# One chained attention, softplus layer and expert layer on one core: another order at the seam between the layers, and the first expert's weights split earlier, one piece a step

## The chip, the cores and the metric

The kernel runs on one core of a Trainium2 chip. The metric is the device time of one execution in microseconds (us). A core has five engines that run their own instruction queues in order and wait for one another by semaphores: PE (TensorE, matrix products), ACT (ScalarE), DVE (VectorE), POOL (GpSimd) and SP, which here does nothing but issue DMAs.

## The reference

Three layers are chained. The first is a gated linear attention: a state of 48 x 48 for each of 8 heads is decayed and updated at each of 768 positions. The second is a two-layer network over 3072 tokens (384 to 2048 and back), with softplus between. The third is a layer of 8 experts, of which each token takes at most one.

```
x = attention(q, k, v, f_logit)                  # 3072 tokens x 384
h = x @ w_in;  g = softplus(h);  x = g @ w_out   # 384 -> 2048 -> 384
do = (x @ w_skip) > 0;  e = argmax(x @ w_gate)   # which tokens, which expert
out = x;  out[do] += prob[e] * (relu(x @ w1[e]) @ w2[e])
```

All products are made to float32's precision: each operand is a high part of reduced precision plus a low part, and each product is three matrix products (high by high, high by low, low by high).

## The kernel before

**Units and steps.** The tokens of the softplus layer go in 12 units of 256. A unit has 8 steps, each for 256 of the 2048 hidden columns, so there are 96 steps, `s` = 0 to 95 (loop at the line `for s in range(-20, total)`). The names in the trace carry the step within the unit: `ph6` of the last unit but one is step 86. A step's work is spread over four engines:

- `up(s)`: 18 matmuls into the PSUM tile `ph` (L396). Two such tiles exist, so `up(s)` waits until `ph` of step s-2 has been read for the last time.
- `act_a(s)`: on ACT absolute value (L411), exponential (L412), plus one (L413); on DVE two operations (L415, L416). L416 is the last reader of `ph`.
- `act_b(s)`: the logarithm on ACT (L422) and a sum on POOL (L423).
- `act_c(s)`: on ACT the high part `gh` (L431), on DVE the low part `gl` (L432).
- `down(s)`: 12 matmuls (L443) from `gh` and `gl` into the accumulators `acc0` and `acc1`. It is put behind `up(s+2)`. Its first matmuls need `gh`, the third or the fifth needs `gl`.

Up to step 85 the attention of the next units runs in between. The last step of the last unit works in halves of 256 columns, with the sum on DVE.

**Routing.** When a unit is through, `Route` copies the accumulators out (L463), writes the output rows and the table `x_s` of rows to DRAM (L464, L490, SP), picks an expert for each token and ranks the tokens by two small matmuls `pr` (L502, L503). The two `scatter` calls (L511) then write token numbers into the DRAM array `table` by indirect DMAs of POOL, the second after the first has landed. For the last unit there is no scatter: `last_rank` and `last_ids` do it on the chip, by `pr`, the one-hot tiles `prow` and `pcol` (L526, L527), the product `pplace` (L533) and the lists `ids`.

**The first expert's tokens.** The expert with the most tokens comes first. Its number is known after step 80 (`set_turns`). `first_ids` reads the first 256 places of its list from `table` into `col` (L602, read on DVE at L604), two gathers of POOL fetch those rows (`xg`, L663), and `firsts.turn` transposes them on PE (`pxg`, L694) and splits them (L373, L374). `firsts` then runs in four steps of `up` (`phm`, L711) and `down` (`pom`, L756) with expert 0's weights, and its `pom` uses the accumulators' PSUM. `table_cols` reads the whole table into `rows` by 8 DMAs (L542) and transposes it on PE (`pids`, L547).

**Expert weights.** An expert has four quarters of 768 KB, numbered `n` = 4e to 4e+3: two of w1, two of w2. `w_load(n)` brings one to SBUF by an SP DMA (L630, `w<-in_moe_w_dram`). `w_split(n)` takes two more slots for its high and low parts, and `w_piece` makes half of a quarter at a time: a cast on ACT (L640) and a subtraction on DVE (L641), both 128 x 768. The raw quarter's slot comes free after its second piece. `wanted` is the list of loads and splits to come, and `feed(n)` starts all of its head for which slots are free and then makes up to `n` pieces.

**What sets the order.** The calls stand in program order, but the build orders each engine's instructions by a schedule of its own, which may hoist work. `pin` keeps an instruction in program order while `pinned` holds something. In the kernel before it does so only from the last unit's routing on, so the pieces of steps 87 to 95 may move.

Of the kernel before, what the change touches and what calls it, by code (L numbers as in the profile page):

```python
# [23 lines left out]
PIECES = 2  # L24
# [13 lines left out]
def gla_softplus_moe_kernel(  # L38
# [17 lines left out]
    NCH, PR, _ = q.shape  # L56
# [14 lines left out]
    STEPS = NF // 2  # L71
# [534 lines left out]


    pools = {"w": mw, "wp": wp}
    slots = [("w", f"w{i}") for i in range(4)]
    raw, w_hi, w_lo, taken = {}, {}, {}, {}  # L610
    pinned = []

# [4 lines left out]
    def w_tile(n, dt):  # L617
        slot = slots.pop(0)
        taken.setdefault(n, []).append(slot)
        return pools[slot[0]].tile([P, KD, F2 // 2] if n % 4 < 2 else [P, NF2 // 2, DM], dt, tag=slot[1], name=f"w{n}", bufs=1)  # L620
# [5 lines left out]
    def w_load(n):  # L626
        e, g = n // 4, n % 4
        raw[n] = w_tile(n, F32)
        src = (w1 if g < 2 else w2)[ds(expert_at[e], 1), g % 2].rearrange("o p c -> (o p) c")
        sy.dma_start(out=raw[n].rearrange("p a c -> p (a c)"), in_=src)  # L630

    def w_split(n):

        w_hi[n], w_lo[n] = w_tile(n, F32R), w_tile(n, F32R)
        return [(n, i) for i in range(PIECES)]
# [9 lines left out]
    wanted, pieces = [], []  # L645

    def feed(n):

        while True:
            while wanted and len(slots) >= (1 if wanted[0][0] == "load" else 2):  # L650
                what, q = wanted.pop(0)
                if what == "load":
                    w_load(q)
                else:
                    pieces.extend(w_split(q))
            if n <= 0 or not pieces:
                return
            w_piece(*pieces.pop(0))
            n -= 1
# [140 lines left out]
    if True:  # L800
        se.preload_act_table_set("natural_log_exp_and_others")
        a_load(0, "fkq")
        a_load(1, "f")
        load_w(0, (0,))
        a_load(1, "kq")
        a_load(0)
        a_load(1)
        load_w(0, (1,))
        load_w(1)
        a_load(2)  # L810
        setup()
        load_wsg()
        clear_routes()
        stages = tuple(zip(("load", "pre", "decay", "transpose", "score", "out"), STAGE_AT))
        todo = {}
        for c in range(NCH):
            for nm, off in stages:
                todo.setdefault(4 * (c + 1) + off - (SOONER[c] if c < len(SOONER) else 0), []).append((c, nm))
        ops = {"load": a_load, "pre": a_pre, "decay": a_decay, "transpose": a_transpose, "score": a_score,
               "out": a_out}  # L820
        order = {nm: i for i, (nm, _) in enumerate(stages)}

        def attention_step(s):
            for c, nm in sorted(todo.pop(s, []), key=lambda x: (x[0], order[x[1]])):
                ops[nm](c)

        routes = {}
        ROUTE = ((1, "evac"), (4, "logits"), (5, "choose"), (6, "rank"), (7, "scatter", 0))
        ROUTE_SOON = ((1, "evac"), (1, "logits"), (2, "choose"), (2, "rank"), (3, "scatter", 0), (3, "scatter", 1))

        def route_step(u, i):
            if u < 0 or u >= NU:
                return
            if i == 1:
                routes[u] = Route(ffns[u], u * UNIT, tid[:, u * CPU:(u + 1) * CPU], *([pools["pre"], cnt_last] if u == NU - 1 else []))
            for at, nm, *a in ROUTE if u < NU - 3 else ROUTE_SOON if u < NU - 1 else ():
                if at == i:
                    getattr(routes[u], nm)(*(a if nm != "rank" else [cnt_acc[:, 0, :]]))
            if i == 2 and 0 < u < NU - 2:
                routes[u - 1].scatter(1)  # L840

        ffns = {}

        def conv(s, j):
            if s in CONV_AT:
                g = CONV_AT.index(s)
                if j % 2:
                    conv_w(g, j // 2)
                if j == 3 and g + 2 < STEPS:
                    load_w(g + 2)  # L850
        total = NU * STEPS
        last_att = 4 * NCH - 2 - STEPS
        for s in range(-20, total):
            u, i = divmod(s, STEPS)
            conv(s, 0)
            if s > 0:
                pu, pi = divmod(s - 1, STEPS)
                ffns[pu].act_b(pi)
            conv(s, 1)
            if s >= 0:  # L860
                if i == 0:
                    ffns[u] = Ffn(xhl[u], FINE if u == NU - 1 else ())
                ffns[u].up(i)
            if s > 0:
                ffns[pu].act_c(pi)
            if s >= 0:
                ffns[u].act_a(i)
            conv(s, 2)
            attention_step(s + STEPS + 1)
            conv(s, 3)  # L870
            if s >= 2:
                pu, pi = divmod(s - 2, STEPS)
                ffns[pu].down(pi)
            route_step(u - 1, i)
            if s == total - 2 * STEPS:
                set_turns()
                for n in range(4):
                    w_load(n)
            if s == last_att:
                first.close()  # L880
                pools["pre"] = rest.enter_context(tc.tile_pool(name="pre", bufs=1, side="right", reuse_waits="tile"))
                slots += [("pre", f"w{i}") for i in range(5)]
                wanted += [("split", n) for n in range(4)] + [("load", n) for n in range(4, 12)] + [("split", n) for n in range(4, 8)]
                for e in range(2, E):
                    wanted += [("split", n) for n in range(4 * e, 4 * e + 4)]
                    if e + 1 < E:
                        wanted += [("load", n) for n in range(4 * e + 4, 4 * e + 8)]
            if u == NU - 1:
                slots.append(("wp", f"s{i}"))
                if pu == u and pi % 2:  # L890
                    slots.extend(("wp", f"s{STEPS + pi - 1 + n}") for n in range(2))
            if s > last_att:
                feed(PIECES if s <= last_att + 4 else 1)
            if s == last_att + 2:
                first_ids()
                firsts = Tiles(0, [id0[:, 0, t:t + 1] for t in range(2)], ("acc0", "acc1"))
                firsts.fetch([id0[:, 1, t:t + 1] for t in range(2)], NT - 2 * UNIT)
            if s == total - 4:
                table_cols()
                last_base()  # L900
            if s == total - 3:
                firsts.turn()
                flags()
# [91 lines left out]
    ffn_end = ffns[NU - 1]  # L995
# [10 lines left out]
    def last_rank():  # L1006
        last.rank(cnt_all)
        last.place()
# [2 lines left out]
        set_ids(last.placed())  # L1011
        flag_counts()

    later = [[(ffn_end.down, STEPS - 2)], [(last_down,)]]
    seq = [(w, i) for w in work for i in range(len(w.steps))]
    fetched, turned = 1, 1
    ffn_end.act_b(STEPS - 1)
    for at in range(len(seq) + 2):
        if at < len(seq):
            w, i = seq[at]  # L1020
            while pieces and pieces[0][0] <= 4 * w.e + (1 if i == 0 else 3):
                w_piece(*pieces.pop(0))
            now, then = w.steps[i]
            for f, *args in now:
                f(*args)
            if at == 0:
                ffn_end.act_c(STEPS - 1)
            turn_at = 0 if w.n == 1 else 3 if w is firsts else 2
        for _ in range(2 if len(later) > 1 and (at == 2 or (at > 2 and w.n == 2 and i)) else 1):
            for f, *args in later.pop(0) if later else ():  # L1030
                f(*args)
        if at < len(seq):
            later += then
        feed(FILL[at])
        if at == 1:
            last_rank()
        elif at == 2:
            last_ids()
        if at >= 2 and at < len(seq):
            k0 = work.index(seq[at][0])  # L1040
            while fetched < len(work) and fetched <= k0 + 1:
                work[fetched].fetch(work[fetched].cols)
                fetched += 1
            if turned == k0 + 1 and turned < fetched and i == turn_at:
                work[turned].turn()
                turned += 1
# [9 lines left out]
    with tc.If(some > 0, preferred_fallthrough_block=False), ExitStack() as gen:  # L1056
# [23 lines left out]
        for e in range(E):  # L1080
            n = nc.values_load(cnt[0:1, e:e + 1], min_val=0, max_val=NT)
            with tc.If(n > 0):
# [6 lines left out]
                with tc.For_i(0, (n + (P - 1)) // P, 1) as it:  # L1089
# [3 lines left out]
                    w = Tiles(e, [c[:, 1:2]], ("acc0",))  # L1093
# [75 lines left out]
```

## Time and profile before

| | us |
|---|---|
| three runs | 750.46, 752.81, 754.51 |
| median | 752.81 |
| the profiled execution | 751.03 |
| its span, first to last instruction | 749.3 |
| PE busy | 688.8 (92%) |
| DVE busy | 538.5 (72%) |
| ACT busy | 477.2 (64%) |
| POOL busy | 199.3 (27%) |

Times in the trace count from the start of the span. An engine's bracket, as in [0.98 <-DVE u L416], says how long it sat idle before the instruction and what ended that. [...]

### The profile page before, as it was taken

To read this page: it belongs to the slowest core of one execution; us is meant where nothing else is said; L and a number is where in the kernel's file an instruction comes from. 1 tells how busy PE (TensorE), PEld (TensorE's weight loads), DVE (VectorE), ACT (ScalarE), POOL (GpSimd) and SP (SyncE) were. 2 spreads that over 40 slices of the span, in tenths; PEclk is the share of its full clock that TensorE was granted. 3 is DMA by queue.
4 is the path that set the end of the run, shared out by engine and by line. 5 is a ranking of instruction groups with operands and counts; after the bars stand their busy time and mean duration, and the time that the engine had idled before them with its cause. 6 is when DMAs were issued, how large, how long until landed. Compare 5 with 4: busy or idle time off the path is not lost. (4 is left out here: it accounts for less than half of the span.)

```text
span 749.3 us, 15063 instructions
## 1 busy us (share of the span) xinstructions
PE 688.8 (92%) x5869; PEld 639.8 (85%) x5869; DVE 538.5 (72%) x1081; ACT 477.2 (64%) x864; POOL 199.3 (27%) x170
## 2 busy tenths in 40 slices
PE   1788889999999999999999999999979979999993
PEld 1576768989999999999999999999969878989893
DVE  6989999867777677778767777756667555866851
ACT  5596777767666766766686666656567634555750
POOL 1204212322222323222232322223333204222111
PEclk9989999999999999999999999999999999999997
DMA  9944423202132121212212121100606412555910
GB/s 278 282 159 147 151 66 111 80 26 74 55 82 73 50 64 52 87 56 76 77 41 70 45 85 44 61 9 1 210 22 219 166 43 82 189 210 198 324 43 11
DMA packets 33905, 77.19 MB, mean 103 GB/s; under 512 B 5967, under 2 KB 18594, under 8 KB 33824
## 3 DMA queue, kind: packets, MB, share of 16 engines
q1 hardware_dynamic: 31456, 71.89, 29.7%
q0 software_dynamic: 2368, 4.25, 2.0%
q8 instruction: 48, 0.79, 0.5%
q14 instruction: 33, 0.27, 0.1%
HBM read 64.89 MB, written 12.11 MB: 103 GB/s over the span
## 5 line engine op out<-in xcount | busy, mean ns | idle before, releaser
L396 PE MATMUL ph<-xh,wi 128*128 128x256 f32 x1152 | 229.1, 288 | 3.2 <-ACT wi L215 1.6
L423 POOL TENSOR_TENSOR w<-w,u 128x512 f32<-128x512 f32 x95 | 129.3, 1361 | 354.0 <-DVE u L416 204.5
L396 PEld LDWEIGHTS ph<-xh,wi 128*128 128x128 f32 x1152 | 187.2, 192 | 8.2 <-ACT wi L215 2.3
L396 PE MATMUL ph<-xl,wi 128*128 128x256 f32 x576 | 163.9, 285 | 0.0
L443 PE MATMUL acc<-wo_hi,gh 128*128 128x394 f32 x384 | 137.8, 360 | 2.2 <-ACT gh L431 2.2
L443 PE MATMUL acc<-wo_hi,gl 128*128 128x394 f32 x384 | 130.1, 346 | 3.8 <-DVE gl L432 3.6
L443 PE MATMUL acc<-wo_lo,gh 128*128 128x394 f32 x384 | 131.7, 343 | 0.0
L396 PEld LDWEIGHTS ph<-xl,wi 128*128 128x128 f32 x576 | 110.8, 192 | 0.0
L432 DVE TENSOR_TENSOR gl<-w,gh 128x512 fp32r<-128x512 f32 (+1 forms) x97 | 67.0, 692 | 43.1 <-ACT gh L431 42.5
L415 DVE SCALAR_TENSOR_TENSOR u<-w,u 128x512 f32<-128x512 f32 (+1 forms) x97 | 66.7, 689 | 34.3 <-ACT w L413 33.9
L411 ACT ACTIVATE u<-ph 128x512 f32<-128x512 f32 (+1 forms) x97 | 56.9, 587 | 46.5 <-PE ph L396 44.9
L422 ACT ACTIVATE w<-w 128x512 f32<-128x512 f32 (+1 forms) x97 | 60.9, 628 | 37.0 <-DVE u L415 36.9
L443 PEld LDWEIGHTS acc<-wo_hi,gh 128*128 128x128 f32 x384 | 72.4, 189 | 7.9 <-ACT gh L431 3.3
L431 ACT CAST gh<-w 128x512 fp32r<-128x512 f32 (+1 forms) x97 | 59.2, 611 | 30.4 <-POOL w L423 26.2
L443 PEld LDWEIGHTS acc<-wo_hi,gl 128*128 128x128 f32 x384 | 72.6, 189 | 5.4 <-DVE gl L432 5.1
L443 PEld LDWEIGHTS acc<-wo_lo,gh 128*128 128x128 f32 x384 | 73.1, 190 | 0.2 <-DVE wo_lo L243 0.2
L416 DVE SCALAR_TENSOR_TENSOR u<-ph,u 128x512 f32<-128x512 f32 (+1 forms) x97 | 65.9, 680 | 3.3
L641 DVE TENSOR_TENSOR w<-w,w 128x768 fp32r<-128x768 f32 x64 | 59.5, 973 | 7.5 <-ACT w L640 4.7
L412 ACT ACTIVATE u<-u 128x512 f32<-128x512 f32 (+1 forms) x97 | 60.7, 627 | 1.6
L413 ACT ACTIVATE w<-u 128x512 f32<-128x512 f32 (+1 forms) x97 | 60.5, 625 | 1.4
L756 PE MATMUL pom<-w,gh 128*128 128x384 f32 x208 | 54.2, 342 | 2.5 <-DVE om L766 2.5
L640 ACT CAST w<-w 128x768 fp32r<-128x768 f32 x64 | 49.8, 837 | 3.1 <-DMA w<-in_moe_w_dram 2.3
(194 smaller groups left out, 1134.6 us busy)
## 6 DMA issues: line engine op xcount, KB each, us to landing
w<-in_moe_w_dram SPq DMA_DIRECT2D x32, 768.0 KB
si<-in_moe_w_in_dram SPq DMA_DIRECT2D x8, 768.0 KB
so<-in_moe_w_out_dram SPq DMA_DIRECT2D x8, 768.0 KB
f<-in_f_logit_dram SPq DMA_DIRECT2D x24, 227.5 KB
q<-in_q_dram SPq DMA_DIRECT2D x24, 224.0 KB
k<-in_k_dram SPq DMA_DIRECT2D x24, 224.0 KB
x_s<-xr SPq DMA_DIRECT2D x24, 192.5 KB
v<-in_v_dram SPq DMA_DIRECT2D x24, 192.0 KB
```

The lines of the kernel that those rows point to most:

```text
L396: te.matmul(ph[:, j, :], lhsT=w[i][:, kk, j * P:(j + 1) * P], rhs=x[:, kk, :], start=(n == 0), stop=(n == 3 * KD - 1))
L411: se.activation(u[:, c], ph[:, c], AF.Abs)
L412: se.activation(u[:, c], u[:, c], AF.Exp, scale=-1.0)
L413: se.activation(w[:, c], u[:, c], AF.Identity, bias=1.0)
L415: ve.scalar_tensor_tensor(u[:, c], w[:, c], 1.0, u[:, c], op0=ALU.subtract, op1=ALU.subtract)
L416: ve.scalar_tensor_tensor(u[:, c], ph[:, c], 0.0, u[:, c], op0=ALU.max, op1=ALU.subtract)
L422: se.activation(w[:, c], w[:, c], AF.Ln)
L423: (ve if i in self.fine else ge).tensor_tensor(w[:, c], w[:, c], u[:, c], op=ALU.add)
L431: se.copy(flat(gh)[:, c], w[:, c])
L432: ve.tensor_tensor(flat(gl)[:, c], w[:, c], flat(gh)[:, c].bitcast(F32), op=ALU.subtract)
L443: te.matmul(self.acc[t][:, 0:XR], lhsT=g[:, j, t * P:(t + 1) * P], rhs=w[f // 4][:, f % 4, :], start=(f == 0 and n == 0), stop=(f == NF - ...
L641: pin(ve.tensor_tensor(lo, t, hi.bitcast(F32), op=ALU.subtract))
```

## The change

Five edits, all at the end of the softplus layer:

1. The four quarters of the first expert are no longer loaded together at step 80. Two are, quarter 0 is split from step 83 on into the slots that quarters 2 and 3 had, and quarters 2 and 3 are loaded as slots come free. The slots of the pool `mw` are handed out in another order for that.
2. Pieces are made one a step: at steps 83 and 85, and at each from 87 to 95 (before: two a step from 87 to 90, then one). They are pinned.
3. `table_cols` and `last_base` stand at step 94 and not 92.
4. `down` of step 94 and `act_c` of step 95 stand ahead of the first expert's first `up`, and not behind it.
5. `last_rank` stands between the first expert's first two `down` steps, and not ahead of its third `up`.

```diff
-    slots = [("w", f"w{i}") for i in range(4)]
+    slots = [("w", f"w{i}") for i in (2, 3, 0, 1)]
...
             if s == total - 2 * STEPS:
                 set_turns()
-                for n in range(4):
-                    w_load(n)
+                wanted += [("load", 0), ("load", 1), ("split", 0), ("load", 2), ("split", 1), ("load", 3)]
+                feed(0)
             if s == last_att:
...
-                wanted += [("split", n) for n in range(4)] + [("load", n) for n in range(4, 12)] + [("split", n) for n in range(4, 8)]
+                wanted += [("split", n) for n in (2, 3)] + [("load", n) for n in range(4, 12)] + [("split", n) for n in range(4, 8)]
...
-            if s > last_att:
-                feed(PIECES if s <= last_att + 4 else 1)
+            if s > total - 2 * STEPS + 1 and (s > last_att or s % 2):
+                pinned.append(True)
+                feed(1)
+                pinned.clear()
...
-            if s == total - 4:
+            if s == total - 2:
                 table_cols()
                 last_base()
...
-    later = [[(ffn_end.down, STEPS - 2)], [(last_down,)]]
+    later = [[], [(last_down,)]]
...
     ffn_end.act_b(STEPS - 1)
+    ffn_end.down(STEPS - 2)
+    ffn_end.act_c(STEPS - 1)
...
-            if at == 0:
-                ffn_end.act_c(STEPS - 1)
...
-        for _ in range(2 if len(later) > 1 and (at == 2 or (at > 2 and w.n == 2 and i)) else 1):
+        for n in range(2 if len(later) > 1 and (at == 2 or (at > 2 and w.n == 2 and i)) else 1):
             for f, *args in later.pop(0) if later else ():
                 f(*args)
+            if at == 2 and n == 0:
+                last_rank()
...
-        if at == 1:
-            last_rank()
-        elif at == 2:
+        if at == 2:
             last_ids()
```

On DVE, steps 85 to 87 (`ph5` to `ph7`), the rows stood like this before; L641 are the pieces of quarters `w0` to `w2`, L604 waits for the read of `col`, L432 is `gl`:

```order
L604 CAST id0_99<-col0_98 128x2
L605 TENSOR_SCALAR id0_99<-col0_98 128x2
L415 SCALAR_TENSOR_TENSOR u_6919<-w_6920,u_6919 128x512
L374 TENSOR_TENSOR xl11_6651<-py23_6926,xh11_6650 128x3x128
L416 SCALAR_TENSOR_TENSOR u_6919<-ph5_6896,u_6919 128x512
L641 TENSOR_TENSOR w0_7062<-w0_6581,w0_7061 128x768 x2
L641 TENSOR_TENSOR w1_7064<-w1_6583,w1_7063 128x768 x2
L641 TENSOR_TENSOR w2_7070<-w2_6585,w2_7069 128x768 x2
L415 SCALAR_TENSOR_TENSOR u_6994<-w_6995,u_6994 128x512
L432 TENSOR_TENSOR gl_6991<-w_6920,gh_6990 128x512
L416 SCALAR_TENSOR_TENSOR u_6994<-ph6_6971,u_6994 128x512
```

Now, at the same place:

```order
L415 SCALAR_TENSOR_TENSOR u_6919<-w_6920,u_6919 128x512
L374 TENSOR_TENSOR xl11_6649<-py23_6926,xh11_6648 128x3x128
L416 SCALAR_TENSOR_TENSOR u_6919<-ph5_6896,u_6919 128x512
L641 TENSOR_TENSOR w0_6586<-w0_6581,w0_6585 128x768
L432 TENSOR_TENSOR gl_6995<-w_6920,gh_6994 128x512
L415 SCALAR_TENSOR_TENSOR u_6998<-w_6999,u_6998 128x512
L416 SCALAR_TENSOR_TENSOR u_6998<-ph6_6975,u_6998 128x512
L604 CAST id0_99<-col0_98 128x2
L605 TENSOR_SCALAR id0_99<-col0_98 128x2
L432 TENSOR_TENSOR gl_7043<-w_6999,gh_7042 128x512
L415 SCALAR_TENSOR_TENSOR u_7046<-w_7047,u_7046 128x512
L416 SCALAR_TENSOR_TENSOR u_7046<-ph7_7023,u_7046 128x512
```

Six pieces in a row have become one, and the read of `col` is waited for a step later, ahead of step 86's `gl` and step 87's first operations.

On SP, from step 80 to 88, two loads used to stand ahead of the read of `col` that now stand right in front of it (`w2`, `w3`). Before:

```order
L630 DMA w0_6581<-in_moe2_w1_dram 128x1536
L630 DMA w1_6583<-in_moe2_w1_dram 128x1536
L630 DMA w2_6585<-in_moe2_w2_dram 128x1536
L630 DMA w3_6587<-in_moe2_w2_dram 128x1536
L464 DMA out_0_dram<-xr_6688 128x384 x2
L490 DMA x_s_75<-xr_6688 128x385 x2
L602 DMA col0_98<-table_76 128x2x1
```

Now:

```order
L630 DMA w0_6581<-in_moe2_w1_dram 128x1536
L630 DMA w1_6583<-in_moe2_w1_dram 128x1536
L464 DMA out_0_dram<-xr_6686 128x384 x2
L490 DMA x_s_75<-xr_6686 128x385 x2
L630 DMA w2_6971<-in_moe2_w2_dram 128x1536
L630 DMA w3_7067<-in_moe2_w2_dram 128x1536
L602 DMA col0_98<-table_76 128x2x1
```

The load of `w2` waits for the slot of `w0`, that is for the second piece of quarter 0 on DVE, and the read of `col` is queued behind it.

On PE at the seam, the last `down` of the softplus layer, the ranking `pr` of the last unit and the first expert's third `up` (`phm2`) stood like this before:

```order
L443 MATMUL acc0_7229<-wo_hi3_121,gl_7597 128x394
L443 MATMUL acc1_7230<-wo_hi3_121,gl_7597 128x394
L502 MATMUL pr_7678<-roh_7663,before_83 128x16
L503 MATMUL pr_7678<-cnt_last_94,ones_82 128x16
L711 MATMUL phm2_7703<-xh_7443,w1_7063 128x256
```

Now the same two ranking rows stand between the first expert's first and second `down`:

```order
L756 MATMUL pom_7702<-w2_7069,gh_7610 128x384
L756 MATMUL pom_7702<-w2_7070,gh_7610 128x384
L756 MATMUL pom_7702<-w2_7069,gl_7611 128x384
L502 MATMUL pr_7715<-roh_7663,before_83 128x16
L503 MATMUL pr_7715<-cnt_last_94,ones_82 128x16
L756 MATMUL pom_7701<-w2_7069,gh_7633 128x384
L756 MATMUL pom_7701<-w2_7070,gh_7633 128x384
```

So 18 matmuls of `phm2` and 12 of `pom` have come between the layer's last `down` and `pr`; 12 of `pom` are left between `pr` and `pplace`, where there were 18 and 24.

## Rows read from the trace of the kernel before

**Rows 1.** Busy time of each engine by stretch: us, PE, PEld, DVE, ACT, POOL, PEclk, DMA share, GB/s.

```profile
600.00:620.00 20.00, 16.39 (x100) 15.81 (x101) 10.00 (x36) 6.37 (x15) 1.29 (x1) 0.91 0.11 40
...
680.00:700.00 20.00, 19.53 (x114) 17.59 (x113) 15.69 (x20) 13.30 (x21) 3.25 (x3) 1.00 0.74 245
```

**Rows 2.** Waits of PE from 500 to 720 us: total, times, longest.

```profile
PE acc L443 <- DVE gl L432: 3.0, 1, 3.0
...
PE pr L502 <- DVE xr L489: 2.4, 1, 2.4
PE acc L443 <- ACT gh L431: 1.6, 2, 1.2
PE phm L711 <- DVE u L416: 1.4, 1, 1.4
PE pids L547 <- DMA rows<-table: 1.3, 1, 1.3
PE ph L396 <- DVE u L416: 1.0, 1, 1.0
```

**Rows 3.** Timeline of PE, steps 86 to 88: start, duration, what, idle before.

```profile
545.66 0.28 PE L396 MATMUL ph<-xh,wi 128*128 128x256 f32 x1
...
547.82 0.34 PE L443 MATMUL acc<-wo_hi,gh 128*128 128x394 f32 x1
...
549.80 0.34 PE L443 MATMUL acc<-wo_hi,gl 128*128 128x394 f32 x1
...
563.94 0.35 PE L443 MATMUL acc<-wo_hi,gh 128*128 128x394 f32 x1
```

**Rows 4.** Timeline of ACT and of DVE in the same stretch.

```profile
545.66 4.50 ACT L640 CAST w<-w 128x768 fp32r<-128x768 f32 x6
...
549.07 0.17 DVE L604 CAST id<-col 128x2 int32<-128x2 f32 x1 [3.41 <-DMA col<-table]
...
550.89 6.58 DVE L641 TENSOR_TENSOR w<-w,w 128x768 fp32r<-128x768 f32 x6
```

**Rows 5.** Timeline of ACT: a logarithm's wait, and the chain of step 89.

```profile
539.69 0.63 ACT L422 ACTIVATE w<-w 128x512 f32<-128x512 f32 x1 [0.91 <-DVE u L415]
...
568.46 0.60 ACT L411 ACTIVATE u<-ph 128x512 f32<-128x512 f32 x1 [0.69 <-PE ph L396]
...
574.61 0.60 ACT L431 CAST gh<-w 128x512 fp32r<-128x512 f32 x1
```

**Rows 6.** Timeline of PE: ranking of the last unit but one, and the seam.

```profile
576.90 0.29 PE L502 MATMUL pr<-roh,before 128*128 128x16 f32 x2
...
612.68 0.36 PE L502 MATMUL pr<-roh,before 128*128 128x16 f32 x2 [2.42 <-DVE xr L489]
...
613.12 0.41 PE L711 MATMUL phm<-xh,w 128*128 128x256 f32 x1
...
616.86 0.51 PE L756 MATMUL pom<-w,gh 128*128 128x384 f32 x2
...
621.07 0.81 PE L533 MATMUL pplace<-pcol,prow 128*128 128x192 f32 x4
```

**Rows 7.** Timeline of DVE behind the last ranking.

```profile
615.09 0.38 DVE L527 TENSOR_SCALAR pcol<-place,rcols,rless 128x192 f32<-128x192 f32 x1
...
619.62 0.69 DVE L721 SCALAR_TENSOR_TENSOR gl<-phm,gh 128x512 fp32r<-128x512 f32 x1 [4.15 <-ACT gh L720]
```

**Rows 8.** The read of `col` on SP, and all DMAs on `table`, from issue to landing.

```profile
544.94 0.40 SPq L602 DMA_DIRECT2D col<-table x1
...
DMA to landing us min/median/max: 2.1/2.8/8.7
```

**Rows 9.** Timeline of POOL: the two scatters of the last unit but one.

```profile
579.42 1.22 POOL L511 DMA_INDIRECT table<-tid,rslot  x1 [0.83 <-DVE rslot L508]
580.66 1.55 POOL L423 TENSOR_TENSOR w<-w,u 128x512 f32<-128x512 f32 x1
586.12 1.02 POOL L511 DMA_INDIRECT table<-tid,rslot  x1 [3.91 <-DMA table<-tid,rslot]
```

## The prediction

> **What bounds the kernel now.** I read the busy time by stretch first. PE is the fullest engine throughout the softplus layer and the experts' part; at the seam between them it is not: from 600 to 620 us it works 16.39 of 20 us, and its clock is down to 0.91 on the mean [rows 1]. So the next view is what PE waits for from 500 to 720 us [rows 2]. Seven waits before and at the seam hold 10.7 us. What a wait costs beyond itself is in the timeline of PE.
>
> *Steps 86 to 88.* An `up` takes 547.82 - 545.66 = 2.16 us. A `down` is 12 rows, the last of which starts 1.98 us behind the first, so 0.18 us a row and 2.16 us in all [rows 3]. From the end of the first `down` (549.98) to the start of the one of step 86 (563.94) there are 13.96 us, and the work in them is two `up` and one `down`, 6.48 us. **7.5 us are lost.** The waits in it are 1.0, 1.2 and 3.0 us [rows 2]; the other 2.3 us are mostly matmuls at half clock behind the last wait. The cause stands on the other engines [rows 4]. DVE first waits 3.41 us for the read of `col`, with step 85's operations behind it, and then makes six subtractions of pieces in a row, 6.58 us. Step 86's operations and step 85's `gl` are queued behind them. ACT has its six casts in a row too, 4.50 us, but the logarithm behind them waits for DVE anyway.
>
> *The seam.* PE waits 1.3 us for the table's `rows`, 1.4 us ahead of `phm`, 0.4 us for `gh` (1.6 us less the 1.2 counted above) and 2.4 us for the ranking of the last unit [rows 2]. Behind the last one the third `phm` takes 616.86 - 613.12 = 3.74 us [rows 6] where 18 matmuls of this shape take 2.16 us [rows 3]: it runs at half clock, and 1.6 us go there.
>
> Together 7.5 + 1.3 + 1.4 + 0.4 + 2.4 + 1.6 = **14.6 us** lie idle or slow that this change touches.
>
> **The change part by part.**
>
> *One piece a step.* The number of pieces up to the first expert is eleven in both orders; only their places change. A piece is 4.50 / 6 = 0.75 us of ACT and 6.58 / 6 = 1.10 us of DVE [rows 4]. On ACT it stands between a step's third activation and the logarithm, where ACT waits 0.91 us for DVE [rows 5]: that wait covers it. On DVE it stands behind the step's second operation, with nothing urgent right behind. From a step's first activation to the end of its `gh` there are 575.21 - 568.46 = 6.75 us [rows 5]; its `down` comes two `up` and two `down` after its `up`, 8.64 us later. If a piece lengthened the chain on both engines, 6.75 + 1.85 = 8.60 us would still about do. I set the cost at nothing, and the 7.5 us go. Without that cover each of the nine steps from 87 to 95 costs up to 1.85 us; that is a rival below.
>
> *The read of `col`.* It is now queued on SP behind the loads of quarters 2 and 3, and the first of these waits for step 85's piece. Take the 3.41 us wait away, and that piece starts on DVE near 550.89 - 3.41 = 547.5 and ends near 548.6 [rows 4]; with two issues in front the read goes out near 549.6, an estimate. It landed 549.07 - 544.94 = 4.1 us after its issue [rows 4, 8]; the slowest DMA on `table` took 8.7 us [rows 8]. So DVE gets it between 553.7 and 558.3. What is queued behind the wait is `gl` of step 86. PE asks for that 5 x 2.16 + 4 x 0.18 us after 545.66, at 557.2 [rows 3], and the two operations and `gl` need 0.9 us, so nothing is late up to 556.3. The cost is 0 to 2.0 us. I take 0, since the read is a small one and the nearest row is its own.
>
> *Two loads in place of four at step 80.* That eases the DMA engines for unit 9's scatters; nothing on PE waits for it. I set it at nothing.
>
> *The table two steps later.* The same 8 reads and two transposes, now behind the first `phm`. In the execution before PE asked for them 1.3 us too soon [rows 2]; now it asks one `up`, a third of a `down` and one `phm` later, 2.16 + 0.72 + 2.16 = 5.0 us. What lets the reads go is the landing of unit 10's second scatter, which no longer has a sum of POOL ahead of it. The 1.3 us go. The 1.4 us ahead of `phm` go with them: `phm` waited there for a step whose activations stood on ACT behind the transposes' casts, and those are now made two to three steps earlier, when the rows have long been gathered.
>
> *`down` of step 94 ahead of the expert's first `up`.* Between the last `up` and its own `down` stand now two `down` and one `phm`, 6.5 us against a chain of halves. The 0.4 us go.
>
> *`last_rank` later.* Let t be the end of the layer's last `down` (612.68 - 2.42 = 610.26 before). `pr` can start at t + 2.4. Now it starts behind `phm2` and 12 of the 24 `pom`: the 24 take 621.07 - 616.86 = 4.2 us [rows 6], so at t + 2.16 + 2.1 = t + 4.3. The wait and the half clock behind it go, 4.0 us. But the cover behind `pr` shrinks. From `pr`'s start to the end of `pcol` DVE needs 615.09 + 0.38 - 612.68 = 2.79 us, and a `gl` of the expert, 0.69 us, now stands between [rows 6, 7]: `pplace` is ready at t + 7.8. PE is through with `pr` (0.44 us) and 12 `pom` at t + 6.8. **A new wait of 0.9 us**, too short for me to count a slow clock behind it.
>
> *The scatters of unit 10.* They now stand back to back on POOL, ahead of the sum of step 91; before, that sum stood between them [rows 9]. The second waits until the first has landed. Count from the end of step 91's `up`. The first scatter starts 579.42 - 576.90 = 2.5 us after the ranking [rows 6, 9]. The landing takes 2.8 us in the median of all DMAs on `table` [rows 8], and 586.12 - 579.42 = 6.7 us here [rows 9]. Then come the second's issue (1.0), the sum (1.5) and `gh` (0.6): 8.4 or 12.3 us. PE wants `gh` after two `up`, two `down` and the ranking and transposes, 8.64 us and an estimate of 1 us. So the cost is 0 to 2.7 us. In the execution before, loads were queued ahead of the scatter; in the new order quarter 6 and all behind it wait on SP for a piece that DVE makes after the ranking. The gap is then nearer to the median, and I take 0.
>
> [...]
>
> **The sum.** 14.6 - 0.9 = 13.7 us less. On the profiled execution's 751.03 us that is 737.3. That execution is 1.8 us under the median of the runs; the four times shown have a mean of 752.2, and I take the gain from that: **738.5 us**. PE has the expert part behind the seam, with 19.53 of 20 us busy at 680 to 700 [rows 1], and every order there is unchanged, so I expect the gain to reach the end whole.
>
> **The rivals.**
>
> *The scatters meet the loads* (0.15). If the gap is 6.7 us, PE waits 2.7 us at `down` of step 91. That is about the length of the wait behind which the third `phm` ran at half clock, so 1.6 us more: 4.3 us, 742.8 us. For it speaks the 6.7 us gap [rows 9], against it that the loads are issued later.
>
> *The expert part does not come forward* (0.10). If the weights' loads and not PE set the pace there, about half the gain is given back, 7 us: 745.4 us. For it speaks a DMA share of 0.74 from 680 to 700, against it PE's 19.53 us in the same row [rows 1].
>
> *A piece a step sits on the path* (0.06). Place: steps 87 to 95, between a step's activations and its `down`. Price: up to 0.75 + 1.10 us for each of nine steps, 16.7 us, more than the 13.7 gained: 755.2 us. It decides from the point at which chain and piece pass 8.64 us; by the row of step 89 they reach 8.60. ACT's own wait of 0.91 us speaks against it [rows 5]. Half the chance of this one I put at over 3.8 us slower.
>
> The forecast has 0.62. The last 0.07 are for waits of a microsecond or two that I have not seen, among them the read of `col`.
>
> **How the numbers follow.** The range starts at the fastest run less all that is idle, 750.46 - 14.6 = 735.9, and a little for the spread of runs: 735.5. It ends at the second rival, 745.5. About half a per cent, 3.8 us, is what a measurement of this kernel can tell from no change. Faster by more: forecast, scatters, the last 0.07 and nearly all of the second rival, 0.92. Slower: 0.03. Same: 0.05.
>
> **What would show it.** Right: pieces on DVE as single rows of about 1 us; no wait of PE over 1 us from step 86 to the seam; no wait of PE for the ranking, and one of about 0.9 us for `pcol` ahead of `pplace`; PEclk 1.00 from 540 to 610 us. Wrong: a wait of PE for `gh` at step 91 behind a long gap of the scatters; DVE held by `col` beyond 556 us; a new wait of some tenths in every step from 87 on; or a seam that comes 14 us sooner with an end that does not.

## The result, and the profile after

The changed kernel takes 739.86 us in the median of six runs (738.59 to 740.91). The kernel before, beside it, takes 752.35 us (750.46 to 754.86). The ratio is 0.9835, with a 95% interval from 0.9813 to 0.9857: 12.5 us less, where 13.7 were forecast. The predicted time was 738.5 us in a range of 735.5 to 745.5.

What PE waits for from 500 to 720 us in the changed kernel (total, times, longest), to be held against [rows 2]:

```profile
PE pom L756 <- DVE om L766: 2.5, 2, 1.8
PE acc L443 <- ACT gh L431: 2.3, 1, 2.3
PE phm L711 <- DVE xl L374: 0.9, 1, 0.9
PE phw L731 <- ACT xh L373: 0.6, 1, 0.6
PE phw L731 <- DVE xl L374: 0.5, 1, 0.5
```

The seven waits of [rows 2] are gone. The other four rows, on `om`, `xl` and `xh`, lie in the experts' part and are the same before and after. One wait is new, 2.3 us for `gh`. The busy windows show where it is (us, PE, PEld, DVE, ACT, POOL, PEclk, DMA share, GB/s; PEclk is the share of TensorE's full clock that was granted):

```profile
540.00:560.00 20.00, 20.00 (x183) 19.67 (x182) 11.26 (x20) 13.26 (x24) 8.35 (x7) 1.00 0.26 90
560.00:580.00 20.00, 20.00 (x143) 19.77 (x142) 16.34 (x40) 16.87 (x32) 6.97 (x5) 1.00 0.51 171
580.00:600.00 20.00, 17.75 (x123) 17.48 (x122) 14.05 (x21) 13.79 (x27) 7.25 (x5) 1.00 0.56 201
600.00:620.00 20.00, 19.38 (x125) 17.80 (x124) 10.22 (x41) 4.67 (x10) 4.08 (x4) 1.00 0.26 80
```

PE is full up to 580 us at full clock (PEclk 1.00), and at the seam it works 19.38 us where it worked 16.39 [rows 1].

**A ruler for the stretches.** Whole executions come to the last attention work up to 4.7 us apart, ahead of all that the change touches; the kernel before and the changed one, 2.35 us apart there, are that far apart already at the second ranking `pr`, at 199.61 and 201.96 us. So I measure between three marks that every kernel has: the last masked copy of the attention (DVE, L327), the ranking of the last unit but one (PE, L502), and the first `phw` (PE, L731), which stands behind the first expert's four `phm`. The marks, for the kernel before (its ranking is in [rows 6], at 576.90):

```profile
537.13 1.37 DVE L327 COPY_PREDICATED a_sb<-causal,pc 128x512 f32<-128x512 uint8 x2 [1.67 <-PE pc L319]
...
627.41 0.73 PE L731 MATMUL phw<-w,xh 128*128 128x512 f32 x2 [0.57 <-ACT xh L373]
```

and for the changed kernel:

```profile
539.48 1.37 DVE L327 COPY_PREDICATED a_sb<-causal,pc 128x512 f32<-128x512 uint8 x2 [0.82 <-PE pc L319]
...
571.76 0.29 PE L502 MATMUL pr<-roh,before 128*128 128x16 f32 x2
...
617.52 0.73 PE L731 MATMUL phw<-w,xh 128*128 128x512 f32 x2 [0.57 <-ACT xh L373]
```

A is from the first mark to the second, B from the second to the third, C from there to the profiled execution's time. All kernels of this study, in us (where the kernel before ran again beside others, its median was 751.9 to 752.7):

| kernel | A: to the ranking | B: seam | C: experts | median of runs |
|---|---|---|---|---|
| before | 39.77 | 50.51 | 123.62 | 752.35 |
| changed | 32.28 | 45.76 | 123.39 | 739.86 |
| changed, again | 32.29 | 46.99 | 125.14 | 742.74 |
| edits 1 and 2 alone | 32.29 | 51.17 | 123.36 | 747.87 |
| edits 3 to 5 alone | 40.23 | 43.69 | 125.29 | 746.30 |
| scatters apart | 32.29 | 43.23 | 125.09 | 738.28 |
| scatters apart, again | 32.29 | 43.29 | 123.69 | 739.25 |
| loads held | 32.29 | 44.59 | 123.55 | 738.02 |
| `col` later (before) | 36.81 | 52.83 | 125.33 | 750.86 |
| edit 5 undone | 32.29 | 51.81 | 123.46 | 746.46 |
| edit 3 undone | 32.29 | 50.82 | 124.95 | 746.87 |
| apart, edit 5 undone | 32.28 | 46.98 | 124.85 | 742.35 |
| apart, edit 3 undone | 32.29 | 51.48 | 123.39 | 746.12 |

One more kernel, one piece a step in the kernel before, has its ranking at another place on PE; its A and B together are 91.53 (before 90.28), its median is 753.57.

So the change gains 39.77 - 32.28 = 7.49 us in A, 50.51 - 45.76 = 4.75 in B and 0.2 in C. The profiled execution itself, 740.91 us against 751.03, shows 10.1 of these 12.5 us, because its first mark comes 2.35 us later.

### The profile page after: what moved, and what is told of

Its sections match the earlier page's. It is cut to its first block, busy times and chain, and to the rows that moved or that the text cites. A ratio compares the mean times of both kernels' runs of the same rounds, so it can differ in the third digit from the quotient of the medians.

```text
span 739.2 us, 15063 instructions
## 1 busy us (share of the span) xinstructions
PE 686.6 (93%) x5869; PEld 639.6 (87%) x5869; DVE 536.0 (73%) x1081; ACT 477.1 (65%) x864; POOL 204.0 (28%) x170
## 5 line engine op out<-in xcount | busy, mean ns | idle before, releaser
L423 POOL TENSOR_TENSOR w<-w,u 128x512 f32<-128x512 f32 x95 | 134.6, 1417 | 348.8 <-DVE u L416 210.3
L432 DVE TENSOR_TENSOR gl<-w,gh 128x512 fp32r<-128x512 f32 (+1 forms) x97 | 68.3, 704 | 46.9 <-ACT gh L431 45.6
L641 DVE TENSOR_TENSOR w<-w,w 128x768 fp32r<-128x768 f32 x64 | 58.6, 952 | 1.9 <-PE phw L731 1.3
```

Source lines behind the costliest of these rows:

```text
L423: (ve if i in self.fine else ge).tensor_tensor(w[:, c], w[:, c], u[:, c], op=ALU.add)
L432: ve.tensor_tensor(flat(gl)[:, c], w[:, c], flat(gh)[:, c].bitcast(F32), op=ALU.subtract)
L641: pin(ve.tensor_tensor(lo, t, hi.bitcast(F32), op=ALU.subtract))
```

## The experiments

**Where the new wait comes from.** In the changed kernel's timeline, POOL (the two scatters and the sum of step 91), SP (the loads) and PE (`down` of step 91):

```profile
575.72 1.49 POOL L511 DMA_INDIRECT table<-tid,rslot  x1 [1.38 <-DVE rslot L508]
581.18 1.00 POOL L511 DMA_INDIRECT table<-tid,rslot  x1 [3.97 <-DMA table<-tid,rslot]
582.19 1.29 POOL L423 TENSOR_TENSOR w<-w,u 128x512 f32<-128x512 f32 x1
...
576.42 6.23 SPq L630 DMA_DIRECT2D w<-in_moe_w_dram  x6
...
584.18 0.45 PE L443 MATMUL acc<-wo_hi,gh 128*128 128x394 f32 x1 [2.25 <-ACT gh L431]
```

The second scatter, which waits for the landing of the first, starts 5.46 us behind it; SP begins to issue six loads in that time, and the sum of step 91 stands behind it all. The first scatter comes late too: 575.72 - 571.76 = 3.96 us behind the ranking, where it was 2.5 before [rows 6, 9]. On DVE the ranking's first operation (L504) waits behind the operations of two steps, with a piece ahead of them, and starts 1.34 us behind `pr`, not 0.55; up to `rslot` (L508), which releases the scatter, another 0.7 us goes to the first tokens' split (L374) and small operations for flags. With edits 1 and 2 alone it is 3.4 us. DVE before:

```profile
577.45 1.17 DVE L504 TENSOR_TENSOR cnt_acc<-cnt_acc,roh 128x8 f32<-128x8 f32 x1 [0.32 <-PE pr L503]
...
578.97 0.17 DVE L508 TENSOR_SCALAR rslot<-rrk 128x2 int32<-128x2 f32 x1
```

and in the changed kernel:

```profile
570.22 0.96 DVE L641 TENSOR_TENSOR w<-w,w 128x768 fp32r<-128x768 f32 x1
...
573.10 1.27 DVE L504 TENSOR_TENSOR cnt_acc<-cnt_acc,roh 128x8 f32<-128x8 f32 x1
...
575.28 0.15 DVE L508 TENSOR_SCALAR rslot<-rrk 128x2 int32<-128x2 f32 x1
```

Two edits test what stands behind the first scatter. The first puts the second scatter behind that sum (for units 9 and 10; unit 9's stood behind a sum already):

```diff
-        ROUTE_SOON = ((1, "evac"), (1, "logits"), (2, "choose"), (2, "rank"), (3, "scatter", 0), (3, "scatter", 1))
+        ROUTE_SOON = ((1, "evac"), (1, "logits"), (2, "choose"), (2, "rank"), (3, "scatter", 0))
...
             route_step(u - 1, i)
+            if u >= NU - 2 and i == 4:
+                with tc.issue_after(ffns[u].sum.ins):
+                    routes[u - 1].scatter(1)
```

`act_b` keeps its sum on POOL (L423) in `self.sum` for that, and `issue_after` queues the scatter behind it.

> The changed kernel with one more edit: the second scatter of unit 10 is queued on POOL behind the sum of step 91. My account: the wait of 2.25 us for gh at down of step 91 is that sum standing behind the second scatter, which waits for the landing of the first. The sum then starts near 578.5 and not at 582.2, the wait goes, and the second scatter starts within half a microsecond of 581.2 all the same: 739.9 - 2.3 = 737.6 us. Rival: gh is late for another reason (ACT's logarithm, the piece on ACT): the wait keeps 1 us or more and the time stays at 739 to 740. Second rival: the wait moves on to the table's rows, which the second scatter releases: 738.5 to 739.9, with a wait for pids.

Measured: 738.28 us (735.45 to 738.88), ratio to before 0.9811 (0.9789 to 0.9834). The wait is gone, B is 2.53 us shorter, and PE has no wait for the table's rows. POOL:

```profile
574.51 1.49 POOL L511 DMA_INDIRECT table<-tid,rslot  x1 [1.37 <-DVE rslot L508]
577.61 1.83 POOL L423 TENSOR_TENSOR w<-w,u 128x512 f32<-128x512 f32 x1 [1.60 <-DVE u L416]
579.96 1.02 POOL L511 DMA_INDIRECT table<-tid,rslot  x1 [0.52 <-DMA table<-tid,rslot]
```

The sum now fills the gap, and the second scatter starts 5.45 us behind the first, as it did. My account held.

The second edit leaves the scatters back to back and moves the six loads behind the reads of the table:

```diff
-        sy.dma_start(out=raw[n].rearrange("p a c -> p (a c)"), in_=src)
+        srcs[n] = src
+        if held and n >= 6:
+            late.append(n)
+        else:
+            w_fetch(n, src)
...
+    def w_fetch(n, src):
+        pin(sy.dma_start(out=raw[n].rearrange("p a c -> p (a c)"), in_=src))
...
             if s == total - 2:
                 table_cols()
                 last_base()
+                held.clear()
+                pinned.append(True)
+                for n in late:
+                    w_fetch(n, srcs[n])
+                pinned.clear()
```

> The changed kernel with the issue of the six loads that stand behind the first scatter of unit 10 (quarters 6 to 11) moved behind the reads of the table's rows; scatters back to back as they are. If loads in flight lengthen the landing of the scatter: from the first scatter's start to the second's 3 to 4 us and not 5.5, the wait at down of step 91 falls from 2.25 to under 0.8 us, and the time is 737.6 to 738.5 as long as the quarters still come in time for the second expert. If the gap is the scatter's own time: it stays at 5 us or more, the wait stays at 2 us, and the time is 739.9 or more. If the quarters come too late, a wait for them stands in the expert part and the end is later than the seam says.

Measured: 738.02 us (737.06 to 740.62), ratio 0.9822 (0.9796 to 0.9848). POOL and PE of this kernel:

```profile
572.88 1.49 POOL L511 DMA_INDIRECT table<-tid,rslot  x1 [1.37 <-DVE rslot L508]
575.76 1.77 POOL L511 DMA_INDIRECT table<-tid,rslot  x1 [1.40 <-DMA table<-tid,rslot]
...
579.56 0.45 PE L443 MATMUL acc<-wo_hi,gh 128*128 128x394 f32 x1 [0.47 <-ACT gh L431]
```

The gap falls from 5.46 to 2.88 us and the wait to 0.47, and C is not longer: the six loads in flight lengthened the landing of this small scatter, by 2.6 us. Unit 9's scatters agree: the second starts 8.93 us behind the first in the kernel before, with four loads ahead of them, and 6.61 us in the changed kernel, with two. B is still 1.4 us longer than with the scatters apart; 0.5 of it is the wait left, and the rest I did not follow.

**Each half alone.** Edits 1 and 2 on the kernel before (the diff stands in the section on the change):

> Edits 1 and 2 alone: early loads and one pinned piece a step; the end of the layer as in the kernel before. My account: the 7.5 us of steps 86 to 88 go, the seam keeps its waits for the table's rows (1.3 us), ahead of phm (1.4) and for the ranking (2.4 with half clock behind it), and POOL has the two scatters of unit 10 back to back, so that down of step 91 waits 2.3 us: 752.4 - 7.5 + 2.3 = 747.2 us. Rival: the seam's waits hang on DMAs that do not come sooner with PE, and grow by what was gained: 750 us or more.

Measured: 747.87 us (745.43 to 749.77), ratio 0.9946 (0.9917 to 0.9974). A is that of the changed kernel to 0.01 us. In B the wait at step 91 is 2.43 us with half clock behind it (PEclk 0.66 from 585 to 590 us), the ranking's wait is 2.4 us, and none is left for the table's rows. The time came out near the 747.2 expected, but by another sum: the waits for the rows (1.3 us) and ahead of `phm` (1.4) were to stay and are gone but for 0.3, the half clock behind the ranking is gone (PEclk 1.00 there), and the half clock behind step 91 and a further wait of 0.9 us for `gh` stand in their place. The rival fell: B is 0.7 us longer than before, and not 7. Edits 3 to 5 on the kernel before:

> Edits 3 to 5 alone: table two steps later, down of step 94 ahead of the expert's first up, ranking later; loads and pieces as in the kernel before. My account: 1.3 + 1.4 + 0.4 + 2.4 + 1.6 = 7.1 us go, steps 86 to 88 lose their 7.5 us as before, and the sum of step 91 stands between the scatters, so there is no wait at down of step 91: 752.4 - 7.1 = 745.3 us. Rival: the seam's edits only pay with the pieces done early, because the burst of pieces leaves ACT and DVE late into the seam: then some of the waits stay, 748 us or more.

Measured: 746.30 us (741.72 to 748.66), ratio 0.9919 (0.9882 to 0.9956). B is 6.8 us shorter, against 7.1 expected, and PE has no wait in the seam. A stays at 40.23. So the two halves are separate causes: apart they take 6.8 and 6.4 us off A and B together, with all edits 12.2.

**What the 7.5 us of A are made of.** First the kernel before with the read of `col` and the gathers one step later, the burst of pieces kept:

```diff
-            if s == last_att + 2:
+            if s == last_att + 3:
                 first_ids()
```

> The kernel before with the reading of the first expert's list (first_ids and the two gathers) moved one step later in the program, so that DVE no longer waits for col ahead of step 85's operations; the burst of six pieces stays. My account of the 7.5 us: the 3.41 us wait for col and the burst add up on DVE. The burst then starts 3.41 us sooner, PE keeps the wait of 3 us for gl with the half clock behind it and loses the two waits of 1.0 and 1.2 us: 749 to 750 us. Rival one, the col wait alone does it (the pieces would be covered without it): all 7.5 us go, 745 us. Rival two, the burst alone does it: 752 us, all three waits stay.

Then one pinned piece a step, with the wait for `col` kept and nothing split early:

```diff
             if s > last_att:
-                feed(PIECES if s <= last_att + 4 else 1)
+                pinned.append(True)
+                feed(1)
+                pinned.clear()
```

> The kernel before with one pinned piece a step from step 87 on in place of two a step from 87 to 90; all four quarters are loaded at step 80 as before, nothing is split early, and the wait for col stays. My account: DVE still waits about 3.4 us for col ahead of step 85's operations, PE loses some 1.5 to 2.2 us of it, and the 3 us wait for gl with its half clock goes; what edits 1 and 2 together gave, less 2 us: 749.5 to 750 us. Rival one, the burst alone does it: as edits 1 and 2 together, 747.9 us, no wait over 0.5 us before step 91. Rival two, the col wait alone does it: 752 us. If the early split of two quarters is needed, the first expert's first up waits for its weights, and a wait of PE for w stands at the seam.

Measured: 750.86 us (745.51 to 754.38), ratio 0.9974 (0.9943 to 1.0005), for the first; 753.57 (750.61 to 759.05), ratio 1.0013 (0.9984 to 1.0042), for the second. The waits of PE from 500 to 575 us, of the first:

```profile
PE acc L443 <- ACT gh L431: 2.7, 1, 2.7
```

and of the second:

```profile
PE acc L443 <- ACT gh L431: 1.5, 2, 1.1
PE ph L396 <- DVE u L416: 1.1, 2, 0.6
```

With the burst alone, A keeps 36.81 - 32.29 = 4.5 us: the wait of 2.7 us and 1.7 us of half clock behind it (PEclk 0.69 and 0.97 in two windows of 5 us). With the wait for `col` alone, PE idles 2.65 us in this stretch (summed over windows of 5 us) and its clock holds (PEclk 1.00). The two make 7.2 of the 7.5 us: both causes add, and neither rival holds. But neither kernel keeps its gain at the seam. The first gives 2.3 of its 3.0 us back in B, where half clock behind the ranking costs 3.5 us (PEclk 0.65 and 0.66 in two windows of 5 us) and cost 1.8 before (0.91 in the 20 us of [rows 1]). The second kernel's time was not what I expected: it gives back more than it gained, by waits of 1.5 and 0.9 us in the layer's last steps, one of 3.7 us for the table's rows, and half clock behind that (PEclk 0.79 and 0.52 in two windows of 5 us). PE came sooner, and the rows came later: 61.07 us behind the first mark, against 56.78 before. No wait of PE for weights appeared.

**Edits 5 and 3 alone.** First edit 5 undone in the changed kernel:

```diff
-            if at == 2 and n == 0:
-                last_rank()
...
-        if at == 2:
+        if at == 1:
+            last_rank()
+        elif at == 2:
             last_ids()
```

> The changed kernel with edit 5 alone undone: last_rank again ahead of the expert's third up. My account: the wait of 2.4 us ahead of pr is back, with half clock behind it worth 1.6 us: 739.9 + 4.0 = 743.9 us; if the clock holds, 742.3. Rival: what PE waits for here is made up later, because pplace then comes sooner and the lists of the next tiles with it: 740 to 741 us.

Then edit 3:

```diff
-            if s == total - 2:
+            if s == total - 4:
                 table_cols()
                 last_base()
```

> The changed kernel with edit 3 alone undone: table_cols and last_base again at step 92. My account in the prediction: the wait of 1.3 us for the rows of the table is back, and up to 1.4 us ahead of phm: 741.2 to 742.6 us. Rival, since edits 1 and 2 alone left no wait for the rows: they removed it and not edit 3, and the time is that of the changed kernel, 739.9 us.

Measured: 746.46 us (740.14 to 746.90), ratio 0.9882 (0.9820 to 0.9944), without edit 5; 746.87 (743.96 to 748.68), ratio 0.9913 (0.9883 to 0.9944), without edit 3. Both are higher than any account had it. In both the wait at step 91 had grown too, to 3.2 and 3.5 us, so I undid the same edits, one at a time, once more with the scatters apart.

> scatter_apart with edit 5 undone (last_rank ahead of the expert's third up), so that the wait of step 91 does not mix in. My account: 2.3 to 2.4 us of waiting ahead of pr and half clock behind it of 1.6 us: 3.9 us over scatter_apart, 742. If rank_back's 746 was more than this wait and the longer one of step 91: 744 or more.

> scatter_apart with edit 3 undone (table_cols at step 92), so that the wait of step 91 does not mix in. The trace of table_back shows, beside the longer wait of step 91, the six transposes pxg of the first tokens standing between the two pids ahead of the first phm and not behind the ranking of step 90, waits of 0.4 us for xh and 1.6 us for gh there, and half clock behind them. If these belong to the table's place: they stay, and with half clock of 1.6 to 2 us the time is 3.5 to 4 us over scatter_apart, 742. If they were a result of the late down of step 91: 738 to 739 us.

Measured: 742.35 us (740.25 to 744.41), ratio 0.9873 (0.9830 to 0.9917), without edit 5, and 746.12 (742.99 to 747.28), ratio 0.9912 (0.9887 to 0.9936), without edit 3. For edit 5 the account holds: 3.1 us in the medians, 3.7 in B, and PE's row is close to the one of before, with its 2.42 us [rows 6]:

```profile
602.63 0.40 PE L502 MATMUL pr<-roh,before 128*128 128x16 f32 x2 [2.32 <-DVE roh L492]
```

Edit 3 is worth 6.9 us in the medians and 8.2 in B, not the 2.7 of the prediction; 746.12 is also neither of the two times expected here, 742 and 738 to 739. Without it, PE, POOL and SP show:

```profile
572.41 0.29 PE L502 MATMUL pr<-roh,before 128*128 128x16 f32 x2
...
581.66 1.02 POOL L511 DMA_INDIRECT table<-tid,rslot  x1 [1.94 <-DMA table<-tid,rslot]
...
588.15 3.92 SPq L542 DMA_DIRECT2D rows<-table  x8
...
592.54 0.39 PE L547 MATMUL pids<-ident,rows 96*128 96x96 f32 x1 [3.52 <-DMA rows<-table]
...
600.66 0.35 PE L711 MATMUL phm<-xh,w 128*128 128x256 f32 x1 [1.16 <-DVE u L416]
...
603.82 0.45 PE L443 MATMUL acc<-wo_hi,gh 128*128 128x394 f32 x1 [0.78 <-ACT gh L431]
```

and in the kernel before:

```profile
590.60 3.90 SPq L542 DMA_DIRECT2D rows<-table  x8
...
593.91 0.27 PE L547 MATMUL pids<-ident,rows 96*128 96x96 f32 x1 [1.33 <-DMA rows<-table]
```

The rows hang on the scatters and the loads. Count from the ranking, 576.90 before [rows 6] and 572.41 here. The second scatter starts 9.2 us behind it in both. The reads of the rows, which wait for its landing, go out at 13.7 before and at 15.7 here, and the rows reach PE at 17.0 and 20.1. PE asks for them at 15.7 and 16.6. So it is the table that comes later behind the ranking, not PE that comes sooner: PE waits 3.5 us instead of 1.3, with 1.7 us of half clock behind (PEclk 0.71 and 0.95 in two windows of 5 us). SP's wait ahead of the reads tells when the second scatter has landed: 4.4 us behind its start before, 6.4 here, 6.7 in the changed kernel and 3.8 with the loads held. So the six loads, which now come behind the first scatter, lengthen this landing too; with edit 3 undone no run holds them. Edit 3 puts PE's asking behind that landing, and so keeps what edits 1 and 2 gain. Edit 4's 0.4 us has no run of its own.

**The two best side by side.**

> The changed kernel as it is, beside the next three on one chip. 739 to 741 us, with the wait of about 2.3 us for gh at down of step 91.

> The same edit as scatter_apart: the second scatter of unit 10 behind the sum of step 91. If that wait was the last thing that the change lost: 2.3 us under the changed kernel of this call. Rival: the executions differ by more than that, and the wait is made up elsewhere: less than 1 us under it.

Measured: 742.74 us (736.69 to 745.60), ratio 0.9876 (0.9832 to 0.9921), for the changed kernel, above the 739 to 741 expected of it but again inside the predicted range, and 739.25 (735.86 to 741.25), ratio 0.9826 (0.9791 to 0.9861), with the scatters apart. The medians differ by 3.5 us, though the intervals overlap. The traces say it more sharply: B is 45.76 and 46.99 us with the scatters back to back, 43.23 and 43.29 with them apart. Its A and B together, 75.5 and 75.6 us, are the shortest of the study.

## Why the prediction was right

- **Steps 86 to 88, 7.5 us.** Right: 7.49. Both causes that it named have a share, 4.5 and 2.65 us. The pieces stand singly on DVE, and none leaves a wait on PE in A:

```profile
548.19 0.94 DVE L641 TENSOR_TENSOR w<-w,w 128x768 fp32r<-128x768 f32 x1
...
555.63 0.17 DVE L604 CAST id<-col 128x2 int32<-128x2 f32 x1 [1.34 <-DMA col<-table]
...
558.49 0.95 DVE L641 TENSOR_TENSOR w<-w,w 128x768 fp32r<-128x768 f32 x1
```

- **The read of `col`, set at 0.** Right. It was issued at 550.25 and came to DVE at 555.63, 5.4 us later, between the bounds of 4.1 and 8.7. Less the 2.35 us by which this execution's first mark is later, that is 553.3, and nothing was late up to 556.3.
- **The seam, 7.1 us.** Right for the five terms together: B falls by 6.8 us with edits 3 to 5 alone, by 7.3 with the scatters apart. Shown one by one, edit 5's 4.0 held as 3.7; edit 3's 2.7 was mis-sized. The term was read from the order before; in the new one, where the table comes later behind the ranking, the same edit is worth 8.2. The sum came out because all edits are made together and the waits go whatever their length.
- **The new wait of 0.9 us at `pplace`.** Too large, and not where I put it:

```profile
608.22 0.29 PE L502 MATMUL pr<-roh,before 128*128 128x16 f32 x2
...
610.60 0.34 PE L756 MATMUL pom<-w,gl 128*128 128x384 f32 x1
610.99 1.08 PE L533 MATMUL pplace<-pcol,prow 128*128 128x192 f32 x4
```

PE starts `pplace` right behind the last `pom`. I let it wait for the end of `pcol`, but its first pair needs the first token tile's half alone. The waits of its weight loads for `pcol` come to 0.6 us in two pieces, inside that row, which takes 1.08 us and took 0.81 [rows 6].
- **The scatters of unit 10, set at 0.** This is the step that failed. The text gave 0 to 2.7 us and took 0, since quarter 6 and all behind it would be issued late. They were issued later, but at 576.42, right behind the first scatter. The wait was 2.25 us here. 7.1 - 2.25 = 4.85 us is the seam's gain, and 4.75 were measured. That is the first rival, which had its place and its price, 2.7 us plus 1.6 of half clock, and a part of its cause: the gap was 5.46 us and not 6.7, but the first scatter started 3.96 us behind the ranking, where the sum had 2.5. With the 2.52 of before [rows 6, 9] the wait would have been near 0.8 us, an estimate (2.25 - 1.44) that no run tests. In the profiled execution of the second measurement the wait came with the half clock:

```profile
581.98 0.44 PE L443 MATMUL acc<-wo_hi,gh 128*128 128x394 f32 x1 [1.99 <-ACT gh L431]
...
582.80 0.28 PE L396 MATMUL ph<-xh,wi 128*128 128x256 f32 x1
...
586.44 0.35 PE L443 MATMUL acc<-wo_hi,gl 128*128 128x394 f32 x1
```

The `up` behind the wait takes 3.64 us, not 2.16. That rival's chance, 0.15, was too low: the trace of before had the gap of 6.7 us, and I gave the order of issue more weight than that row.
- **What the loads cost the scatter.** The gap was 5.46 us with the six loads issued behind the first scatter and 2.88 with them held, so they made its landing longer. Through what they did so, no run shows.
- **The other rivals** fell. The experts' part came forward whole (C 123.62 and 123.39), and of the steps from 87 on PE waits at step 91 alone. A piece may have a part there, in the 1.44 us by which the first scatter starts later.
- **The total.** In part luck: 0.9 us were counted at `pplace` and hardly came, and 2.25 us at step 91 came and were not counted. The range held, but it takes in the first rival's 742.8 us as well, so it does not tell the two apart; the wait in the trace does.

## What to carry to other kernels

Size an edit in the order it will stand in, not in the kernel where something else holds the engine up: edit 3 was worth 2.7 us by the old waits and 8.2 us in the new order, where the table came later behind the ranking. When a queue holds a DMA that waits for another DMA, look at what stands behind it: here a sum that PE needed came ready in the gap, and putting it between the two scatters took 2.5 us off the seam, and no wait came up in return. And measure between marks inside the program: with edits 1 and 2 in, A repeats to 0.01 us in ten profiled executions that differ by several as a whole. B and C repeat less well (45.76 and 46.99 us for one kernel's B), for the reason that follows.

## What the runs showed that I had not expected

One and the same wait is followed by half clock in one execution and by full clock in another. In the experts' part PE waits 1.8 us for `om` in every kernel. With the scatters apart, first run:

```profile
661.66 0.62 PE L756 MATMUL pom<-w,gh 128*128 128x384 f32 x2 [1.76 <-DVE om L766]
...
660.00:665.00 5.00, 3.33 (x13) 0.77 0.32 75
665.00:670.00 5.00, 5.00 (x35) 0.89 0.79 302
```

Second run, where PEclk stays at 1.00 from 640 to 680 us:

```profile
664.06 0.62 PE L756 MATMUL pom<-w,gh 128*128 128x384 f32 x2 [1.76 <-DVE om L766]
```

C takes two values by this, 123.4 to 123.7 and 124.9 to 125.3 us, and each of the longer ones has PEclk 0.96 from 640 to 680. The wait of step 91 does the same: full clock behind 2.25 us in the first profiled execution of the changed kernel (PEclk 1.00 from 580 to 590 us), half clock behind 1.99 us in the second (0.80 and 0.86 in two windows of 5 us); with edit 3 undone even 3.48 us there are followed by full clock (PEclk 1.00 from 580 to 590 us). The ranking's wait of 2.4 us has both too: half clock behind it in the kernel before (PEclk 0.50 from 614 to 616 us), full clock with edits 1 and 2 alone (PEclk 1.00 from 610 to 625 us). So in these runs a wait of about two microseconds cost either itself or 1.6 to 1.8 us more, with `col` later 3.5, and executions of one kernel differed by that. What decides between the two is open. The forecast counted half clock only behind the waits where the trace of before happened to show it.
